# Single loads between GpSimd's copies, earlier weight sums and interleaved exponentials in a fused attention and feed-forward kernel

## The chip, the cores and the metric

The kernel runs on one core of a Trainium2 chip. A core has TensorE (PE, matrix products; PEld is its weight load), VectorE (DVE), ScalarE (ACT), GpSimd (POOL) and SyncE (SP, which here only issues transfers), and 16 DMA engines that all queues share. Time is device time of one execution in microseconds, the median of several runs. A profile is one execution of its own, recorded with every instruction.

## The reference

Attention over 8 batches, 12 heads, 448 tokens and head size 64, then a feed-forward layer over the 3584 tokens. Inputs and output are float32; the kernel works in bfloat16 on the inside.

```python
scores = scale * np.matmul(q, k.transpose(0, 1, 3, 2))
scores = scores - np.max(scores, axis=-1, keepdims=True)
attn = np.exp(scores)
attn = attn / (np.sum(attn, axis=-1, keepdims=True) + 1e-09)
attn_out = np.matmul(attn, v)
x = attn_out.transpose(0, 2, 1, 3).reshape(B * S, H * D)      # 3584 x 768
h = x @ w_in                                                  # 768 x 2048
g = np.maximum(0.01 * h, h)
out = g @ w_out                                               # 2048 x 768
```

## The kernel before

**Units.** Attention is cut into 48 units: two heads of one batch each, six units to a batch. For a unit, q, k and v are loaded as bf16 by GpSimd's queue (`load_soft`, line 137; one load brings two units of one of q, k, v into one of two tiles `fq`, `fk`, `fv`), copied by GpSimd into their places (`cast`, line 162: q and k into a tile `qkb`, v into `v`), and q and k are turned (transposed) into `qkT`: for units below 15 by PE and a copy on DVE (`transposes`, line 250, copy on line 263), later by transposing DMAs in SP's queue (`turn`, line 239). Keys come in four chunks of 112, so a unit has four chunks; chunk 54, say, is unit 13's third. A *burst* (line 788) is the scores of three chunks on PE, one into each of three PSUM slots `sc`, and three exponentials on ACT (`expo`, line 281). `rows` (line 759) multiplies a unit's exponentials with v, and DVE divides (lines 774, 775) into `x`, which is turned into `xT`: by PE and DVE for units 9 to 11 (line 321), by SP's queue for the others.

**Feed-forward.** Tokens go in seven blocks, cut at `cuts` (line 41). The later blocks use a Strassen-like scheme with seven products instead of eight, in `hidden` (x times w_in, line 440) and `block_pair` (h times w_out, line 520). It needs sums and differences of the weights, made once on DVE: `mix_w_in` (line 377; 12 differences, an empty step, 4 additions; called `ins`) and `mix_weights` (line 359; 16 differences and sums; called `outs`). Each is a generator: a `next` puts one more of them into DVE's queue. `mix_h` (line 430) makes two such operations on the hidden values h.

**The stage around the change.** The first block has 640 tokens and is computed in the plain way. `head` (line 591) does 448 of them: 16 groups m of six matmuls into one of two PSUM banks `g`, each followed by a Prelu on ACT (line 600). `neck` (line 611) does the other 192: eight groups of twelve matmuls with a Prelu each (line 651). `second(0)` (line 902) then does the block's products with w_out, with `block_pair`'s steps x counted 0 to 15 in each of two pairs c. After each step `place` (line 846) puts attention work between: by a clock of its own it estimates when a PSUM slot is free (line 877) and then emits a burst, a unit's rows or a turn on PE. A burst in head and neck also calls `feed` (line 826), which emits GpSimd's copies of one unit's q and k, then v's that are owed (`pay`), then the loads that have become allowed (`fetch`), then SP's turn of a unit. In head and neck a burst is `lazy`: its third exponential is kept in `late` and goes out after the next Prelu (`settle`, line 339). All engines run their queues in order. After every copy of units from 12 on, GpSimd writes one element to a tile `gate` (line 174).

Of the kernel before, what the change touches and what calls it, by code (L numbers as in the profile page):

```python
# [16 lines left out]
def kernel(  # L17
# [9 lines left out]
    nc = tc.nc  # L27
# [4 lines left out]
    HP = H // 2  # L32
# [129 lines left out]
    def cast(u, parts=(0, 1, 2), by=nc.gpsimd.tensor_copy):  # L162
        if u >= NU:
            return
        for x in parts:
            f = raw[u].pop(x)
            if x < 2 and u not in qk_sb:
                qk_sb[u] = cast_pool.tile([SC, 2, NSC, 2, D], BF16, name="qkb")
            if x < 2:
                by(qk_sb[u][:, x].rearrange("p so h d -> p h so d"), f)  # L170
            else:
                by(v_sb[u % NV][:, :, :, :D], f)  # L172
            if u >= 2 * HP:
                nc.gpsimd.memset(gate[:, :1], 0.0)

    w_steps = []
    for i in range(4):
        w_steps.append((w_in_sb[:, :, ts(i, DF // 4)], w_in_v[:, :, ts(i, DF // 4)]))
# [157 lines left out]

    late = []

    def settle():
        while late:  # L340
            expo(*late.pop(0))

    open_t = {}
    opened = (0, 1)
# [246 lines left out]
    def head(ins, outs):  # L591

        for m in opened:
            part(0, m, (KD - 1,))
        for m in range(MD):
            if m not in opened:
                part(0, m, range(KH))
                yield KH * HEAD / 2400, False
                part(0, m, range(KH, KD))
            nc.scalar.activation(h[:, m, :HEAD], open_t.pop(m)[:, :HEAD], AX.Prelu, alpha=0.01)  # L600
            settle()
            if m == opened[-1]:
                slots.append(idle)
            if m >= 4:
                next(ins)
            if m >= 14:
                next(outs)
                next(outs)
            yield (KH if m not in opened else 1) * HEAD / 2400, True

    def neck(outs):

        n = cuts[1] - HEAD
        at = place_of(HEAD)
        ms = [x + y for x in range(0, MH, 2) for y in (0, MH)]
        held = {}

        def part2(m, kks):
            fresh = m not in held
            if fresh:  # L620
                held[m] = next_bank()
            for j in range(2):
                for kk in kks:
                    nc.tensor.matmul(  # L624
                        held[m][:, j * n:(j + 1) * n], w_in_sb[:, kk, ts(m + j, P)], xT[:, kk, at:at + n],
                        start=(fresh and j == 0 and kk == 0), stop=(kk == KD - 1), skip_group_check=True,
                    )

        assert all(u == need[1] - 1 for u, _ in owed_x), owed_x
        def after(x):  # L630
            if x % 2:
                mix_h(0, ms[x - 1])
            for _ in range((1, 1, 1, 1, 1, 1, 1, 1)[x]):
                next(outs)

        for m in ms[:2]:
            part2(m, range(KD - 1))
        yield 4 * (KD - 1) * n / 2400, False
        for x, m in enumerate(ms):
            if x < 2:  # L640
                assert rows_done >= need[1], rows_done
                settle_x()
                part2(m, (KD - 1,))
                if x:
                    after(x - 1)
            else:
                part2(m, range(KH))
                after(x - 1)
                yield 2 * KH * n / 2400, False
                part2(m, range(KH, KD))  # L650
            nc.scalar.activation(
                h[:, m:m + 2, HEAD:cuts[1]], held.pop(m)[:, :2 * n].rearrange("p (m t) -> p m t", m=2), AX.Prelu, alpha=0.01
            )
            settle()
            yield 2 * (KH if x > 1 else 1) * n / 2400, True
        model["free"][id(slots[0])] = model["now"] + 1.5
        transposes(NPE - 1, next_slot()[:, 0])
        after(len(ms) - 1)
# [72 lines left out]
    sums, more = mix_w_in(), mix_weights()  # L731
    chunk = 4 * HP + 3
    rows_done = HP
    to = {"pe": HP + 2, "turn": NPE, "cast": HP + 4, "v": HP + 4, "load": [HP + 8] * 3}
    tick = 0

    def advance():
# [47 lines left out]

        return u < to["pe"] or to["pe"] == NPE and u < to["turn"]

    def burst(lazy=False):
        nonlocal chunk
        todo = [divmod(chunk + x, NSC) for x in range(3) if chunk + x < NU * NSC]  # L790
        assert rows_done > todo[-1][0] - NE and turned(todo[-1][0]) and to["v"] > rows_done
        for a, c in todo:
            scores(a, c)
        for a, c in todo[:2] if lazy else todo:
            expo(a, c)
        if lazy:
            late.extend(todo[2:])
        chunk += len(todo)

    X_PE = (HP + 3, HP + 4, HP + 5)  # L800
# [9 lines left out]

    ahead = 0

    def fetch():
        for x, y in enumerate(("cast", "cast", "v")):
            u = to["load"][x]
            if u <= ahead and u - 3 < to[y]:
                load_soft(u, 2, (x,))
                to["load"][x] += 2

    def pay():  # L820
        while owed_v and owed_v[0] < rows_done + NV:
# [4 lines left out]
    def feed(g):  # L826
        nonlocal ahead
        t, r = divmod(g, 4)
        u = 3 * t
        if r < 3:  # L830
            cast(u + 3 + r, (0, 1))
            owed_v.append(u + 3 + r)
            to["cast"] = u + 4 + r
        pay()
        if r < 3:
            ahead = u + 5 + r
            fetch()
            load_w({9: 1, 10: 3}.get(g, 0))
        if r > 0:
            dma_transposes(u + 2 + r)  # L840
            to["turn"] = max(to["turn"], u + 3 + r)
# [1 line left out]
    plan = [9, 8, 8, 8, 8, 5, 0]  # L843
    model = {"now": 0.0, "act": 0.0, "free": {}, "ready": {}}

    def place(i, want, soon=0, full=True, calm=True, first=False, lazy=False, keen=NU, cap=NU):

        free, ready = model["free"], model["ready"]
        done, state = 0, 0
        while True:  # L850
            settle_x(model["now"])
            now = model["now"]
            last = divmod(chunk + 2, NSC)[0]
            blocked = rows_done <= min(last, NU - 1) - NE
            u = rows_done
            whole = u < chunk // NSC
            at = [free.get(id(x), 0.0) for x in slots]
            u = to["pe"]
            if full and max(want, soon) > done and u <= min(last, NPE - 1) and state == 0:
                transposes(u)  # L860
                to["pe"] += 1
                state = 1
                model["now"] += 0.45
                continue
            if want > done and state < 2 and turned(last) and not blocked and len(slots) == 3 and all(
                x <= now + 0.05 + 0.2 * j for j, x in enumerate(at)
            ):
                state = 2
                order = list(slots)
                start = chunk  # L870
                burst(lazy)
                if first:
                    feed(start // 3)
                done += 1
                for x, t in enumerate(order[:chunk - start]):
                    model["act"] = max(model["act"], now + 0.45 + 0.2 * x) + 0.8
                    free[id(t)] = model["act"] + (0.65 if lazy and x == 2 else 0.15)
                    if (start + x) % NSC == NSC - 1:
                        ready[(start + x) // NSC] = model["act"] + 0.1
                model["now"] = now + 0.78  # L880
                continue
            u = to["pe"]
            if first and full and state == 0 and u < min(NPE - 1, to["cast"] - 1) and u - NQ < chunk // NSC and model["act"] <= now + 0.6:
                transposes(u)
                to["pe"] += 1
                state = 1
                model["now"] += 0.45
                continue
            u = rows_done
            if calm and whole and not (lazy and late) and at[0] <= now + 0.05 and ready.get(u, 0) <= now + 0.05 and (  # L890
                u <= (chunk + 5) // NSC - NE or u < keen
            ) and u < cap:
                t = slots[0]
                rows()
                if first:
                    pay()
                model["now"] = now + 1.08
                free[id(t)] = now + 2.33
                continue
            return done  # L900

    def second(i):
# [4 lines left out]
        for c in range(len(spots(i)[1])):  # L907
            for x, _ in enumerate(block_pair(i, c)):
# [3 lines left out]
                    model["now"] += 0.65  # L912
                left -= place(i, left, calm=x not in (1, 3), keen=need[min(i + 2, NR)], cap=NU if all(summed) else need[i + 2])
                if i == 0 and x % 2:
                    next(outs if c == 0 and x < 12 else ins, None)
                for y in range(2):
                    if fresh[y] is None and i + 1 < NR and rows_done >= need[i + 2] - 1 + y:
                        fresh[y] = model["now"] + 7.0
# [15 lines left out]
    for steps, aims, cost in ((head(ins, outs), early, 0.55), (neck(outs), goals, 0.5)):  # L934
        groups = 0
        base = len(early) if aims is goals else 0
        for used, full in steps:
# [2 lines left out]
                groups += 1  # L940
                model["act"] = max(model["act"], model["now"]) + cost
            soon = base + sum(x <= groups + 1 for x in aims) - done if full else 0
            done += place(0, base + sum(x <= groups for x in aims) - done, soon, first=True, lazy=True, full=full, keen=NU if aims is goals or groups > 13 else 0)
    settle()
    assert done == len(early) + len(goals), (done, chunk, rows_done)
    assert to["pe"] == NPE - 1, to
# [44 lines left out]
```

## Time and profile before

| what | value |
| --- | --- |
| runs | 394.15, 394.39, 396.0 us, median 394.39 |
| profiled execution | 392.24 us, of which the span of instructions is 390.4 |
| granted TensorE clock | 1.00 throughout |
| busy | PE 378.1, ACT 265.2, DVE 235.0, POOL 143.4 us |
| head, neck, first output stage | about 31 to 64, 64 to 76, 76 to 110 us |
| GpSimd's copy, its load issue, its memset | 0.62-0.70, 0.70, 0.10 us each |

The span runs from the first to the last instruction; the execution's time is a little longer. A row of a timeline gives start, duration, engine, line, operation, output and inputs, shapes and the number of instructions merged; square brackets show how long the engine had stood idle before it and what ended the wait. A duration on DVE or POOL includes time in which the operation was held up inside the engine.

### The profile page before, as it was taken

The numbers are of one execution on the slowest core, as the hardware profiler recorded it, in microseconds if no ns is written. First come the engines' busy times: TensorE is split into PE (matmuls) and PEld (weight loads), VectorE is DVE, ScalarE is ACT, GpSimd is POOL, SyncE is SP. The second block draws the span as 40 slices with busy tenths as digits, with TensorE's granted clock in tenths as the row PEclk, the third lists the DMA queues.
The fourth block names the chain that finished last, engine by engine and source line by source line (L and its number), as shares of the span: only waits on it lengthen the run. The fifth ranks groups of instructions, "written<-read, shape, count | busy, mean of one in ns | idle before, by whom it ended". The sixth has DMA issues, their size and how long they took to land.

```text
span 390.4 us, 10108 instructions
## 1 busy us (share of the span) xinstructions
PE 378.1 (97%) x4086; PEld 259.3 (66%) x4086; DVE 235.0 (60%) x494; ACT 265.2 (68%) x391; POOL 143.4 (37%) x330
## 2 busy tenths in 40 slices
PE   8899998879999999999999999999999999999996
PEld 3565656755678655886557865579755796568854
DVE  3662636895665745667459574575745666464853
ACT  6998884747678777677765877667867677708700
POOL 8798730976247142460426404354042000000000
PEclk9999999999999999999999999999999999999999
DMA  9999999898999929991399912899228610421023
GB/s 135 199 200 204 170 180 189 100 162 127 181 130 148 128 49 165 184 168 28 71 155 177 165 26 50 174 177 147 35 57 166 138 27 3 106 52 55 3 76 87
DMA packets 93247, 46.75 MB, mean 120 GB/s; under 512 B 51856, under 2 KB 89872, under 8 KB 93200
## 3 DMA queue, kind: packets, MB, share of 16 engines
q0 software_dynamic: 38224, 22.58, 44.5%
q1 hardware_dynamic: 54912, 23.50, 31.8%
q8 instruction: 32, 0.52, 0.6%
q14 instruction: 15, 0.12, 0.1%
q10 hardware_dynamic: 64, 0.02, 0.0%
HBM read 45.61 MB, written 11.01 MB: 145 GB/s over the span
## 4 chain that ended last, share of the span: by engine, by line
PE 87%; DVE 4%; DMA 4%; ACT 2%; issue 1%; POOL 1%; DVEq 0%; POOLq 0%; ACTq 0%
PE g L537 31%; PE g L465 14%; PE sc L465 14%; PE sc L768 11%; PE sc L274 9%; PE g L354 3%; DMA xT<-x 2%; DMA w_in_mix<-in_k_dram 2%; PE g L293 2%; PE g L624 1%; ACT e L283 1%; PE g L257 1%; DVE hmix L437 1%; POOL w_in_mix L141 1%; PE sc L354 1%
## 5 line engine op out<-in xcount | busy, mean ns | idle before, releaser
L283 ACT ACTIVATE e<-sc 112x896 bf16<-112x896 f32 x192 | 162.9, 918 | 51.1 <-PE sc L274 51.0
L537 PEld LDWEIGHTS <-h 128*128 128x128 bf16 x680 | 61.3, 98 | 49.0 <-issue 13.8
L537 PE MATMUL g<-w_out_sb,h 128*128 128x384 bf16 x448 | 84.6, 326 | 0.0
L454 ACT ACTIVATE h<-c 128x512 bf16<-128x512 f32 (+1 forms) x72 | 43.5, 611 | 25.2 <-DVE c L480 16.5
L465 PEld LDWEIGHTS <-w_in_sb 128*128 128x128 bf16 x576 | 54.3, 98 | 6.4 <-issue 0.5
L170 POOL COPY qkb<-fq 112x512 bf16<-112x512 bf16 x38 | 24.2, 637 | 78.5 <-DMA fq<-in_q_dram 40.4
L274 PE MATMUL sc<-qkT 64*128 64x448 bf16 x384 | 49.9, 353 | 2.7 <-DVE qkT L263 2.4
L768 PEld LDWEIGHTS <-e 112*128 112x128 bf16 x1344 | 46.6, 98 | 8.4 <-ACT e L283 6.7
L768 PE MATMUL sc<-v,e 112*128 112x65 bf16 x1344 | 50.1, 194 | 0.3 <-ACT e L283 0.3
L172 POOL COPY v<-fv 112x512 bf16<-112x512 bf16 x38 | 23.6, 624 | 68.4 <-PE sc L768 68.3
L465 PEld LDWEIGHTS <-w_in_mix 128*128 128x128 bf16 x432 | 41.2, 98 | 4.1
L537 PE MATMUL g<-w_mix,h 128*128 128x384 bf16 (+1 forms) x224 | 41.6, 323 | 1.3 <-DVE o L542 1.3
L542 DVE COPY o<-g 128x384 f32<-128x384 f32 x53 | 29.3, 554 | 18.9 <-PE g L537 18.3
L545 DVE TENSOR_TENSOR o<-o,g 128x384 f32<-128x384 f32 x42 | 23.1, 551 | 19.3 <-PE g L537 19.3
L774 DVE RECIPROCAL rec<-sc 112x8 f32<-112x8 f32 x42 | 8.7, 207 | 42.8 <-PE sc L768 41.7
L274 PEld LDWEIGHTS <-qkT 64*128 64x128 bf16 x384 | 15.0, 94 | 28.8 <-issue 18.9
L170 POOL COPY qkb<-fk 112x512 bf16<-112x512 bf16 x38 | 26.5, 697 | 17.4 <-DMA fk<-in_k_dram 17.4
L775 DVE TENSOR_TENSOR x<-sc,rec 112x512 bf16<-112x512 f32 x42 | 29.0, 691 | 1.5
L465 PE MATMUL g<-xT,w_in_sb 128*128 128x256 bf16 (+1 forms) x216 | 28.5, 268 | 0.2 <-DVE o L545 0.2
L465 PE MATMUL sc<-xT,w_in_sb 128*128 128x256 bf16 (+1 forms) x216 | 28.5, 268 | 0.0
L537 PE MATMUL g<-w_mix,hmix 128*128 128x384 bf16 x112 | 21.4, 327 | 0.0
L465 PE MATMUL sc<-x_mix,w_in_mix 128*128 128x256 bf16 (+1 forms) x144 | 19.0, 268 | 0.0
(100 smaller groups left out, 471.2 us busy)
## 6 DMA issues: line engine op xcount, KB each, us to landing
fq<-in_q_dram POOLq DMA_DIRECT2D x19, 224.0 KB, 5.9
fk<-in_k_dram POOLq DMA_DIRECT2D x19, 224.0 KB, 6.3
fv<-in_v_dram POOLq DMA_DIRECT2D x19, 224.0 KB, 5.8
w_in_sb<-in_moe_w_in_dram POOLq DMA_DIRECT2D x4, 768.0 KB, 11.5
w_out_sb<-in_moe_w_out_dram POOLq DMA_DIRECT2D x4, 768.0 KB, 19.3
out_dram<-o SPq DMA_DIRECT2D x7, 336.0 KB, 3.3
out_dram<-o SPq DMA_DIRECT2D x8, 288.0 KB, 3.6
out_dram<-o SPq DMA_DIRECT2D x7, 240.0 KB, 3.2
```

Of the source, the lines that this page charges most:

```text
L170: by(qk_sb[u][:, x].rearrange("p so h d -> p h so d"), f)
L172: by(v_sb[u % NV][:, :, :, :D], f)
L274: nc.tensor.matmul(ps[:, j, :S], t[j * D:(j + 1) * D, S + c * SC:S + c * SC + P], t[j * D:(j + 1) * D, :S], start=True, stop=True,)
L283: nc.scalar.activation(e[:, :, c, :], sc_t.pop((u, c))[:SC, :, :S], AX.Exp, scale=scale)
L354: nc.tensor.matmul(open_t[m][:, :n], w_in_sb[:, kk, ts(m, P)], xT[:, kk, at:at + n], start=(fresh and kk == kks[0]), stop=(kk == KD - 1),)
L454: nc.scalar.activation(hs[:, m:m + 2, cols], x.rearrange("p (m t) -> p m t", m=2), AX.Prelu, alpha=0.01)
L465: nc.tensor.matmul(ps[:, j * nh:(j + 1) * nh], w[:, kk, ts(j, P)], x[:, kk], start=(first and j == 0 and kk == 0), stop=(kk == KH - 1), sk ...
L537: nc.tensor.matmul(ps[:, cols], x[:, m], w[:, m], start=(first and m == 0), stop=(m == MH - 1), skip_group_check=True,)
L542: by(o[:, at], ps[:, :NW])
L545: nc.vector.tensor_add(o[:, at], o[:, at], ps[:, :NW])
L768: nc.tensor.matmul(ps[:, j, qc, :], e[:, at:at + P], vt[:, j, c, :], start=(c == 0), stop=(c == NSC - 1),)
L775: nc.vector.tensor_mul(x_t[u].rearrange("p q j d -> p j q d"), ps[:SC, :, :, :D], rec.to_broadcast([SC, 2, NSC, D]))
```

## The change

1. `cast` loses the write to `gate`.
2. `feed` emits q's copy, then at most one allowed load, then k's copy, then at most one. q's progress has its own counter `to["q"]`, so a load of q needs only q's copies. From burst 16 of the count in `feed` (the neck's two bursts) the loads are allowed one unit sooner (`ahead`). In effect the loads of units 18 and 19 come after the copies of q, k and v of unit 15 instead of three in a row after those of unit 16.
3. The w_in differences go to the middle of groups m = 5 to 10, two each (before: one after each Prelu from m = 4). The w_out sums start in the middle of m = 13 (1, 2, 2) and go on with 2, 2, 1, 1, 2, 1, 1, 1 in the neck (before: 2, 2 after the Prelus of m = 14 and 15, one per step in the neck, four in `second(0)`). Standing in the middle of a group, they come behind the copies of turned q and k that follow the group before. `second(0)` has only the w_in additions left, from its first steps.
4. In the neck a burst emits one exponential and keeps two; each Prelu lets one out. The planner counts the second and third slot as taken longer.

```diff
@@ cast
             else:
                 by(v_sb[u % NV][:, :, :, :D], f)
-            if u >= 2 * HP:
-                nc.gpsimd.memset(gate[:, :1], 0.0)
@@
-    def settle():
-        while late:
+    def settle(n=3):
+        while late and n:
             expo(*late.pop(0))
+            n -= 1
@@ head
                 part(0, m, range(KH))
+                for _ in range(2 if 5 <= m < 11 else 0):
+                    next(ins)
+                for _ in range({13: 1, 14: 2, 15: 2}.get(m, 0)):
+                    next(outs)
                 yield KH * HEAD / 2400, False
...
             settle()
             if m == opened[-1]:
                 slots.append(idle)
-            if m >= 4:
-                next(ins)
-            if m >= 14:
-                next(outs)
-                next(outs)
@@ neck
-            for _ in range((1, 1, 1, 1, 1, 1, 1, 1)[x]):
+            for _ in range((2, 2, 1, 1, 2, 1, 1, 1)[x]):
                 next(outs)
...
-            settle()
+            settle(1)
@@
-    to = {"pe": HP + 2, "turn": NPE, "cast": HP + 4, "v": HP + 4, "load": [HP + 8] * 3}
+    to = {"pe": HP + 2, "turn": NPE, "q": HP + 4, "cast": HP + 4, "v": HP + 4, "load": [HP + 8] * 3}
@@ burst
-        for a, c in todo[:2] if lazy else todo:
+        assert not late
+        for a, c in todo[:3 - lazy]:
             expo(a, c)
-        if lazy:
-            late.extend(todo[2:])
+        late.extend(todo[3 - lazy:])
@@ fetch
-    def fetch():
-        for x, y in enumerate(("cast", "cast", "v")):
+    def fetch(n=3):
+        for x, y in enumerate(("q", "cast", "v")):
             u = to["load"][x]
-            if u <= ahead and u - 3 < to[y]:
+            if n and u <= ahead and u - 3 < to[y]:
                 load_soft(u, 2, (x,))
                 to["load"][x] += 2
+                n -= 1
@@ feed
         if r < 3:
-            cast(u + 3 + r, (0, 1))
+            if g >= 16:
+                ahead = u + 6 + r
+            for x, y in enumerate(("q", "cast")):
+                cast(u + 3 + r, (x,))
+                to[y] = u + 4 + r
+                fetch(1)
             owed_v.append(u + 3 + r)
-            to["cast"] = u + 4 + r
         pay()
         if r < 3:
-            ahead = u + 5 + r
+            ahead = max(ahead, u + 5 + r)
             fetch()
@@ place
-                    free[id(t)] = model["act"] + (0.65 if lazy and x == 2 else 0.15)
+                    free[id(t)] = model["act"] + (0.15, 0.15 + 0.5 * (lazy > 1), 0.15 + 0.5 * lazy)[x]
@@ second
-                    next(outs if c == 0 and x < 12 else ins, None)
+                    next(ins, None)
@@ around head and neck
-            done += place(..., lazy=True, ...)
+            done += place(..., lazy=2 if aims is goals else 1, ...)
```

More of the change, by code (lines that the diff above doesn't have):

```diff
@@ L786, in turned, with burst @@
         return u < to["pe"] or to["pe"] == NPE and u < to["turn"]
-    def burst(lazy=False):
+    def burst(lazy=0):
         nonlocal chunk
@@ L844, with place @@
     model = {"now": 0.0, "act": 0.0, "free": {}, "ready": {}}
-    def place(i, want, soon=0, full=True, calm=True, first=False, lazy=False, keen=NU, cap=NU):
+    def place(i, want, soon=0, full=True, calm=True, first=False, lazy=0, keen=NU, cap=NU):
         free, ready = model["free"], model["ready"]
@@ L942 @@
             soon = base + sum(x <= groups + 1 for x in aims) - done if full else 0
-            done += place(0, base + sum(x <= groups for x in aims) - done, soon, first=True, lazy=True, full=full, keen=NU if aims is goals or groups > 13 else 0)
+            done += place(0, base + sum(x <= groups for x in aims) - done, soon, first=True, lazy=2 if aims is goals else 1, full=full, keen=NU if aims is goals or groups > 13 else 0)
     settle()
```

## The prediction

> **What bounds the kernel now.** The page comes first. TensorE (PE) is busy 97% of a span of 390.4 us, no other engine over 68%, so only PE's idle time, 390.4 - 378.1 = 12.3 us, can be won.
>
> ```profile
> PE 378.1 (97%) x4086; PEld 259.3 (66%) x4086; DVE 235.0 (60%) x494; ACT 265.2 (68%) x391; POOL 143.4 (37%) x330
> ```
>
> The table by stretches then says where it lies. Its columns are the stretch, its length, busy time (and instructions) of each engine, granted clock, DMA share and GB/s.
>
> ```profile
> 55.00:60.00 5.00, 4.57 (x71) 3.02 (x72) 2.64 (x7) 3.11 (x5) 0.00 (x0) 1.00 1.19 176
> 60.00:65.00 5.00, 4.25 (x56) 3.12 (x53) 4.33 (x11) 1.09 (x2) 0.00 (x0) 1.00 1.20 207
> 65.00:70.00 5.00, 4.32 (x48) 3.41 (x47) 3.10 (x7) 3.94 (x7) 1.75 (x5) 1.00 0.81 110
> 75.00:80.00 5.00, 3.26 (x32) 1.91 (x30) 4.79 (x7) 3.03 (x5) 5.00 (x12) 1.00 0.99 106
> 80.00:85.00 5.00, 3.71 (x52) 2.31 (x50) 4.83 (x8) 2.84 (x4) 3.09 (x9) 1.00 1.39 199
> 160.00:200.00 40.00, 40.00 (x437) 28.94 (x434) 24.44 (x48) 28.81 (x44) 13.64 (x35) 1.00 0.75 123
> ```
>
> From 55 to 85 us PE idles 0.43 + 0.75 + 0.68 + 1.74 + 1.29 = 4.9 us; from 160 on it idles almost nowhere. The rest is at both ends. PE's timeline of that stretch names the waits, in square brackets:
>
> ```profile
> 59.45 1.10 PE L768 MATMUL sc<-v,e 112*128 112x65 bf16 x29 [0.34 <-ACT e L283]
> 64.00 1.98 PE L624 MATMUL g<-xT,w_in_sb 128*128 128x192 bf16 x22 [0.76 <-DVE qkT L263]
> 68.55 1.84 PE L624 MATMUL g<-xT,w_in_sb 128*128 128x192 bf16 x18 [0.64 <-ACT h L651]
> 78.94 0.36 PE L274 MATMUL sc<-qkT 64*128 64x448 bf16 x2 [1.74 <-DVE qkT L263]
> 83.32 0.81 PE L537 MATMUL g<-w_mix,h 128*128 128x384 bf16 x4 [1.28 <-DVE o L542]
> ```
>
> The last four, 0.76 + 0.64 + 1.74 + 1.28 = 4.42 us, are what the change touches. VectorE's (DVE's) timeline shows what its copies queued behind:
>
> ```profile
> 61.80 0.55 DVE L388 TENSOR_TENSOR w_in_mix<-w_in_sb,w_in_mix 128x768 bf16<-128x768 bf16 x1
> 62.27 0.55 DVE L366 TENSOR_TENSOR w_mix<-w_out_sb 128x768 bf16<-128x768 bf16 x1
> 62.85 0.56 DVE L368 TENSOR_TENSOR w_mix<-w_mix,w_out_sb 128x768 bf16<-128x768 bf16 x1
> 63.33 0.62 DVE L263 COPY qkT<-g 128x896 bf16<-128x896 bf16 x1
> ...
> 74.64 2.23 DVE L437 TENSOR_TENSOR hmix<-h 128x512 bf16<-128x512 bf16 x1
> ...
> 78.26 0.62 DVE L263 COPY qkT<-sc 128x896 bf16<-128x896 bf16 x1
> ...
> 81.24 0.54 DVE L371 TENSOR_TENSOR w_out_sb<-w_out_sb 128x768 bf16<-128x768 bf16 x1
> 81.70 1.09 DVE L549 TENSOR_TENSOR h<-h 128x1024 bf16<-128x1024 bf16 x1
> 82.72 0.54 DVE L542 COPY o<-g 128x384 f32<-128x384 f32 x1
> ```
>
> Two things: sums of 0.47 us net stand ahead of copies that PE waits for, and the L437 at 74.64, which takes 0.42 us elsewhere, took 2.23 because GpSimd (POOL) copied without a break from 73.05 to 76.60.
>
> **Sums of weights (lines 591-634, 914).** The 12 w_in sums go two at a time to m = 5..10, and end near 50 us instead of 64.6. They need the third and fourth quarter of w_in; the fourth was issued at 30.11 and took 12.2 us, so it is there at 42.3, before the seventh sum (about 45). DVE has 4.06 us idle before 54.10: cost nothing; without that idle time it is 0.47 each.
>
> The w_out sums start at m = 13 instead of 14: one, two, two, then 2, 2, 1, 1, 2, 1, 1, 1 in the neck. At 61.8 no sum is left ahead of the copy: it would run there instead of at 63.33, and the 0.76 would go. But the first sum now reaches DVE's head near 55.9 and needs the second quarter of w_out, which was issued at 40.59:
>
> ```profile
> w_out_sb<-in_moe_w_out_dram POOLq DMA_DIRECT2D x1, 768.0 KB, 17.9
> ```
>
> It lands at 40.59 + 17.9 = 58.5. Three sums then run to about 60.1, and behind them wait the reciprocal (59.12 before) and product for unit 10, whose x PE transposes at 60.39. That product ends near 61.0 instead of 60.0, PE's transposes slip 0.6, unit 11's and m = 15 follow. So of the 0.76 I take 0.1, with 0 and 0.76 as ends (an arrival 1 us later would cost 1 more).
>
> In the first output stage the four sums at 81.24, 83.19, 86.11, 87.88 are gone and the w_in additions come at steps 3, 5, 7, 9; the sum before L549 (0.46 us) has no successor.
>
> **Exponentials (lines 339, 654, 788-798, 877).** ACT ran two exponentials (66.40, 1.72 us) before the second Prelu (68.00), which frees the bank for the 68.55 matmuls. One now runs before it: Prelu near 67.2, PE ready at 67.8. From then Prelu 0.40 + exponential 0.82 alternate against PE groups of 1.03 us; following both leaves one wait of 0.08 for the fifth group. I take 0.56 of the 0.64 (0 to 0.64). The planner moves two things as its slots stay taken 0.5 and 1.0 us longer: after the first half of the fifth group the third slot is 0.71 ahead of its clock where 0.45 is let through (before 0.21), so the burst 51-53 goes half a group later, and unit 12's rows one group later (one exponential still owed). PE has other work in both places: nothing on PE. Unit 12's x now stands between the two mix_h and two sums on DVE, about 1.5 us before the copy of unit 14.
>
> **Loads, copies, memset (lines 173, 813-842).** Each of 108 memsets goes; copies 0.59 apart become 0.55 apart: 0.035 x 108 = 3.8 us of POOL, which is 37% busy and waits 68.3 us for PE and 95 us for DMAs. Cost and gain nothing beside PE; it is on the path only from 67.8 to 81. There the order was q14 k14, loads, v13, load, v14, q15 k15 v15 q16 k16, three loads, v16. Now unit 18's loads come after q15, k15 and v15, each 0.70 plus a wait for the copy just ahead, whose tile it overwrites (the row of such a load: 0.26, at 72.35). So k15 ends near 75.8 (was 74.84), k16 near 79.6 (76.60), k17 near 81.3 (80.9): the turns of 15 and 16, in SP's queue in the order 15, x of 12, 16, 17, go out at 75.8 and 79.6 (74.86 and 78.15). Unit 18's q comes sooner, which ends POOL's wait at 81.43. In exchange DVE finds 0.96 us without a copy three times between 74 and 78.4. L437 for the fifth pair starts near 71.6-72.2, against one copy instead of three; the copy of unit 14 then runs near 75.1-75.7, as PE reaches its third scores near 76.1. Wait of 1.74: gone, 1.7; if POOL still holds L437 up for two copies it is 0.55-1.1 less, so 0.6 to 1.74. At L549/L542, PE would ask near 79.1; DVE's chain mix_h, one sum, L549, L542 from 75.7 with one blocked copy ends near 78.7. Take 1.2 of 1.28 (0.4 to 1.28).
>
> [...]
>
> **Sum.** 0.1 + 0.56 + 1.7 + 1.2 = 3.56 us by 83 us. Later places may take some back. Unit 16's turn is needed near 87.5 (second chunk of the burst at 90.86, so 91.1, less 3.6); sent at 79.6 with the 7.0 us it took before it lands at 86.6, 0.9 early. Turns took between 3.8 us (that of 15) and 9.0 (after 97): 0 to 1.1 lost. At the start of the second block DVE waits until 108.96 for a turned x sent at 101.09 (7.9 us), then joins, then PE starts at 110.12. It will be sent near 97.4, behind the turn of 21; with 7.9 us PE starts near 106.4, 3.7 sooner; with 9.6 us (the longest turn between 70 and 130) 2.0 sooner. I take 0.36 off: net 3.2. Profiled: span 387.2, time 392.24 - 3.2 = 389.0. That execution was 2.15 below the median 394.39; on the median's scale 391.2.
>
> **The rivals.** *The second block holds the gain back.* The turned x lands where it did, since the loads of 22 (95.59 and 96.29, landing after 8.0 and 10.0 us) fill the DMA engines. For: DMA share 1.15 there; against: 0.71 and 0.88 in 85-95, room to move up. Gain 0 to 2.0: 393.4. *The w_out arrival or POOL's copies eat it*: w_out 1 us later (-1), L437 and L549 still blocked (-0.8): gain 1.4, 393.0. For: 2.23 in the row; against: loads now break POOL's run. *Slower*: the turn of 16, behind POOL's three loads and waits, comes so late that PE stands at burst 63-65. It costs one for one from 87.5, wipes out the gain if it lands at 91.1, and is 0.5% slower from 93.1, 13.5 us after being sent. For: loads of 14 took 19.2-20.2 us behind w_out; against: no turn in 70-130 took over 9.6. If it lands at 95: 394.4 + 3.9 = 398.3. *No effect*, gain 0: needs all four waits to be replaced; nothing speaks for it.
>
> **How the numbers follow.** The forecast 0.60 (its own range 390.0 to 392.2); second block 0.18; w_out or copies 0.12; slower 0.07; no effect 0.03. A measurement of this kernel tells about 0.5%, 2.0 us. Faster takes the forecast, a third of w_out or copies, a quarter of second block: 0.69; slower 0.08; same 0.23. Low: all 4.42 us and 0.4 for the runs' own spread (394.15 to 396.0), 389.6; high: the second block's 0 with nothing won, 394.3.
>
> **What would show it.** DVE with a wait for w_out near 56-58.5 and L624 starting near 63.9; the neck's ACT row alternating L651 and L283; L263 for unit 14 before 76 and no wait over 0.3 at its scores; L542 before 79.2; PE's first L465 near 106.4. Wrong if L437 is again over 1.5 us, if PE waits for a turn (qkT) near 87, or if L465 starts at 110.

## The result, and the profile after

The changed kernel takes 392.23 us, the kernel before 394.35 (medians of 22 executions each, taken in turn): ratio 0.9952, 95% interval 0.9933 to 0.9972. (The ratio is made of fast executions alone, without one of the changed kernel at 395.96 us, and is not the quotient of the medians.) That is 2.1 us by the medians; the forecast was 3.2, and 391.2 on a scale where the kernel before had 394.39.

The two profiled executions hardly differ: 392.14 us against 392.24, spans 390.2 and 390.4. So the profile has to be read for two things: where the 3.56 us expected by the third product went, and why the medians moved when the profiles did not.

From the table by stretches of the changed kernel (stretch, length, busy time and instructions of PE, PEld, DVE, ACT, POOL, then granted clock, DMA share, GB/s):

```profile
60.00:65.00 5.00, 4.40 (x54) 3.33 (x51) 4.64 (x12) 1.09 (x2) 0.00 (x0) 1.00 1.23 206
65.00:70.00 5.00, 4.97 (x56) 3.90 (x55) 3.13 (x7) 4.30 (x8) 2.64 (x4) 1.00 0.64 85
75.00:80.00 5.00, 2.44 (x13) 0.81 (x11) 4.76 (x10) 2.50 (x4) 4.68 (x6) 0.84 1.38 128
80.00:85.00 5.00, 5.00 (x52) 2.62 (x51) 3.47 (x6) 2.25 (x4) 4.11 (x6) 0.81 0.94 161
```

The neck (65 to 70) has become full. But 75 to 80 holds less PE work than before (2.44 against 3.26 us), and the granted clock, 1.00 everywhere in the profile before, is 0.84 and 0.81. PE's timeline of the changed kernel, with the waits in brackets:

```profile
63.64 1.98 PE L621 MATMUL g<-xT,w_in_sb 128*128 128x192 bf16 x22
66.22 3.50 PE L621 MATMUL g<-xT,w_in_sb 128*128 128x192 bf16 x38
...
75.48 0.36 PE L271 MATMUL sc<-qkT 64*128 64x448 bf16 x2
77.76 0.36 PE L271 MATMUL sc<-qkT 64*128 64x448 bf16 x2 [1.92 <-DVE x L772]
78.77 0.56 PE L271 MATMUL sc<-qkT 64*128 64x448 bf16 x2 [0.64 <-DVE qkT L260]
79.25 3.38 PE L535 MATMUL g<-w_out_sb,h 128*128 128x384 bf16 x12
82.57 0.74 PE L271 MATMUL sc<-qkT 64*128 64x448 bf16 x6
83.24 0.82 PE L535 MATMUL g<-w_mix,h 128*128 128x384 bf16 x4
```

PE starts the neck at 63.64 (64.00 before), runs through it without the 0.64, and is at the scores of the burst 54-56 at 75.48 instead of 76.65: 1.17 us won. There it waits 1.92 us for unit 12's x, whose slot chunk 55 needs, and 0.64 for the copy of unit 14: 2.56 in place of 1.74. Then twelve matmuls that took 2.12 us before take 3.38; before, their row was

```profile
79.23 2.12 PE L537 MATMUL g<-w_out_sb,h 128*128 128x384 bf16 x12
```

The wait of 1.28 before the third product is gone, and the product starts at 83.24 instead of 83.32. Microsecond by microsecond the clock shows why the twelve took longer:

```profile
77.00:78.00 1.00, 0.24 (x2) 0.09 (x1) 0.98 (x2) 0.00 (x0) 1.00 (x2) 1.00 1.35 117
78.00:79.00 1.00, 0.36 (x4) 0.10 (x2) 1.00 (x3) 0.79 (x1) 1.00 (x2) 0.72 1.78 94
79.00:80.00 1.00, 1.00 (x5) 0.41 (x4) 0.90 (x3) 0.77 (x2) 1.00 (x2) 0.50 1.55 126
80.00:81.00 1.00, 1.00 (x5) 0.47 (x4) 0.92 (x2) 0.28 (x1) 0.26 (x1) 0.50 1.43 191
81.00:82.00 1.00, 1.00 (x6) 0.45 (x4) 1.00 (x3) 0.00 (x0) 0.85 (x2) 0.57 1.36 226
82.00:83.00 1.00, 1.00 (x10) 0.40 (x8) 0.70 (x2) 0.00 (x0) 1.00 (x2) 1.00 0.92 199
```

PE's pause begins at 75.84; the clock falls near 78.4, with two matmuls in between, and is back near 81.9: 3.4 us at 0.50. VectorE's timeline shows why unit 12's x was late; its reciprocal could have started when PE's rows ended near 73.5, and started at 76.79:

```profile
58.41 0.56 DVE L364 TENSOR_TENSOR w_mix<-w_out_sb 128x768 bf16<-128x768 bf16 x1 [2.61 <-DMA w_out_sb<-in_moe_w_out_dram]
...
71.73 1.80 DVE L366 TENSOR_TENSOR w_mix<-w_mix,w_out_sb 128x768 bf16<-128x768 bf16 x1
73.45 0.55 DVE L369 TENSOR_TENSOR w_out_sb<-w_out_sb 128x768 bf16<-128x768 bf16 x1
73.92 1.09 DVE L435 TENSOR_TENSOR hmix<-h 128x512 bf16<-128x512 bf16 x1
75.11 0.87 DVE L436 TENSOR_TENSOR h<-h 128x512 bf16<-128x512 bf16 x1
75.91 0.95 DVE L369 TENSOR_TENSOR w_out_sb<-w_out_sb 128x768 bf16<-128x768 bf16 x1
76.79 0.19 DVE L771 RECIPROCAL rec<-sc 112x8 f32<-112x8 f32 x1
```

and GpSimd's timeline beside it what held the sums up:

```profile
71.94 0.62 POOL L172 COPY v<-fv 112x512 bf16<-112x512 bf16 x1
72.48 0.62 POOL L170 COPY qkb<-fq 112x512 bf16<-112x512 bf16 x1
73.40 0.70 POOL L141 DMA_DIRECT2D fq<-in_q_dram  x1 [0.30 <-POOL qkb L170]
74.10 0.62 POOL L170 COPY qkb<-fk 112x512 bf16<-112x512 bf16 x1
```

The sum at 71.73 lasts until 73.53, 0.43 after the second of two copies; the L435 at 73.92 until 75.01, 0.3 after the next one. Elsewhere they take 0.55 and 0.42. It isn't always VectorE that stands: a later copy of GpSimd's is stretched from 0.62 to 1.19 us while VectorE's product and sum at 77.02 and 77.63 run at their usual 0.69 and 0.55.

```profile
77.45 1.19 POOL L170 COPY qkb<-fq 112x512 bf16<-112x512 bf16 x1
```

### The profile page after: what moved, and what is told of

It reads as the page before. It is cut to its first block, busy times and chain, and to the rows that moved or that the text cites. A ratio compares the mean times of both kernels' runs of the same rounds, so it can differ in the third digit from the quotient of the medians.

```text
span 390.2 us, 10005 instructions
## 1 busy us (share of the span) xinstructions
PE 379.7 (97%) x4086; PEld 259.9 (67%) x4086; DVE 234.7 (60%) x494; ACT 265.2 (68%) x391; POOL 139.0 (36%) x222
## 4 chain that ended last, share of the span: by engine, by line
PE 81%; DMA 9%; DVE 4%; POOL 2%; issue 1%; ACT 1%; DVEq 0%; POOLq 0%; ACTq 0%
PE g L535 34%; PE g L463 13%; PE sc L463 13%; PE sc L765 10%; PE sc L271 8%; DMA w_out_sb<-in_moe_w_out_dram 5%; DMA fk<-in_k_dram 3%; DMA w_in_mix<-in_k_dram 2%; POOL qkb L170 1%; PE g L290 1%; POOL w_in_mix L141 1%; ACT e L280 1%; DVE w_mix L364 1%; DVE w_mix L366 1%; PE g L254 0%
## 5 line engine op out<-in xcount | busy, mean ns | idle before, releaser
L535 PE MATMUL g<-w_out_sb,h 128*128 128x384 bf16 x448 | 85.8, 330 | 0.0
L172 POOL COPY v<-fv 112x512 bf16<-112x512 bf16 x38 | 24.6, 651 | 68.7 <-PE sc L765 68.5
L540 DVE COPY o<-g 128x384 f32<-128x384 f32 x53 | 29.3, 554 | 20.5 <-PE g L535 19.9
L170 POOL COPY qkb<-fk 112x512 bf16<-112x512 bf16 x38 | 24.6, 648 | 21.6 <-DMA fk<-in_k_dram 21.6
L463 PE MATMUL g<-x_mix,w_in_mix 128*128 128x256 bf16 (+1 forms) x144 | 19.0, 268 | 0.0
```

What stands on the lines that cost most here:

```text
L463: nc.tensor.matmul(ps[:, j * nh:(j + 1) * nh], w[:, kk, ts(j, P)], x[:, kk], start=(first and j == 0 and kk == 0), stop=(kk == KH - 1), sk ...
L535: nc.tensor.matmul(ps[:, cols], x[:, m], w[:, m], start=(first and m == 0), stop=(m == MH - 1), skip_group_check=True,)
L540: by(o[:, at], ps[:, :NW])
```

## The experiments

After the result: theory A says that the sums and mix_h queued ahead of unit 12's reciprocal and unit 14's copy, held up by GpSimd's copies, made PE wait, and that the pause lowered the clock. Rival B says that unit 12's rows come too late because the planner moved them a group back. Ratios below are to the kernel before, run in turn with each.

**The sums put back** (label u_sums).

```diff
-                for _ in range(2 if 5 <= m < 11 else 0):
-                    next(ins)
-                for _ in range({13: 1, 14: 2, 15: 2}.get(m, 0)):
-                    next(outs)
...
+            if m >= 4:
+                next(ins)
+            if m >= 14:
+                next(outs)
+                next(outs)
...
-            for _ in range((2, 2, 1, 1, 2, 1, 1, 1)[x]):
+            for _ in range((1, 1, 1, 1, 1, 1, 1, 1)[x]):
...
-                    next(ins, None)
+                    next(outs if c == 0 and x < 12 else ins, None)
```

> The changed kernel with the weight sums back in their old places (one w_in difference after each Prelu from m = 4, w_out sums from m = 14, four of them in the first output stage); loads, copies and exponentials as changed. Theory A (in the changed kernel VectorE is late at the end of the neck because sums and mix_h stand ahead of unit 12's reciprocal while GpSimd copies): the wait of 1.92 us on x of unit 12 shrinks to under 1.0, and the waits at the first L621 (0.76) and at the third product (up to 1.3) return; time 392.0 to 393.2. Rival B (unit 12's rows come one group too late through the kept exponentials): the wait of 1.9 stays, the others come on top; 393.3 to 394.4.

392.68 us (12 executions), 0.9952 (0.9921 to 0.9982): within A's span, and not to be told from the changed kernel. There was no wait on unit 12's x, 0.64 for unit 14's copy, and 0.8 each at the neck's first matmuls and at the third product, which started at 81.84. From the neck's first matmul to the third product this run takes 17.10 us, the changed kernel 19.60, of which 1.3 are the lower clock. So the new order of the sums won 0.8 us at the neck and lost more than that behind it. PE's timeline also shows the first rival of the prediction, the second block:

```profile
110.66 1.42 PE L463 MATMUL g<-xT,w_in_sb 128*128 128x256 bf16 x6 [2.24 <-DVE o L543]
```

Behind this wait the clock is at 0.50 again, from 110.7 to 114.1 (0.83 in the mean of 110 to 120).

**The exponentials put back** (u_lazy).

```diff
-            settle(1)
+            settle()
...
-            done += place(..., lazy=2 if aims is goals else 1, ...)
+            done += place(..., lazy=1, ...)
```

> The changed kernel with the neck's exponentials as before (two at once, one kept, all let out at the next Prelu); everything else as changed. A: unit 12's rows stand a group earlier, its x is ready in time, but the copy of unit 14 is still behind mix_h and sums, so PE waits 1 to 2 us there in place of the 1.92 + 0.64, and 0.64 at the Prelu returns: 392.0 to 392.9. B: the wait at the scores after 75 us is under 0.5 us and the kernel gains 1.5: 390.4 to 391.2.

394.24 us (12), 1.0018 (0.9990 to 1.0046): 2.0 us more than the changed kernel by the medians, 2.6 by the ratios, above both expectations. B falls: with the rows a group earlier PE waits longer. VectorE's timeline of this run, then PE's:

```profile
77.38 2.46 DVE L372 TENSOR_TENSOR w_mix<-w_out_sb,w_mix 128x768 bf16<-128x768 bf16 x1
79.77 0.61 DVE L260 COPY qkT<-sc 128x896 bf16<-128x896 bf16 x1
```

```profile
80.43 0.36 PE L271 MATMUL sc<-qkT 64*128 64x448 bf16 x2 [4.04 <-DVE qkT L260]
```

The last sum ahead of unit 14's copy met a run of three copies (77.70 to 79.43) and took 2.46 us; at 77.63 in the changed kernel it took 0.55. With the exponentials as changed the reciprocal and product of unit 12, which PSUM feeds (0.19 and 0.69 us in both runs), stand between the sums, and the run of copies begins at 77.45, beside the product, with the stretched copy of 1.19. So what the exponentials are worth hangs on where VectorE's queue meets GpSimd's; the 0.64 at the Prelu is the smaller part.

**The loads put back, three in a row** (u_loads).

```diff
-            if g >= 16:
-                ahead = u + 6 + r
-            for x, y in enumerate(("q", "cast")):
-                cast(u + 3 + r, (x,))
-                to[y] = u + 4 + r
-                fetch(1)
+            cast(u + 3 + r, (0, 1))
             owed_v.append(u + 3 + r)
+            to["cast"] = u + 4 + r
```

with `fetch` as before.

> The changed kernel with the loads three in a row after the copies of unit 16, as before; no memset. A: GpSimd copies without a break again, VectorE is held up longer between 72 and 76, PE waits 2.5 to 4 us in all at the scores of the burst 54-56: 392.8 to 394.0. B: no difference to the changed kernel within 0.5: 391.8 to 392.7.

393.91 us (12), 0.9979 (0.9944 to 1.0013). The median is in A's span, but the interval overlaps that of the changed kernel, so the time alone does not decide; the trace does. One VectorE operation of 0.55 us stood for 4.00, over six copies that followed each other without a load, and ended at 76.24, 0.46 after the first load's issue began. VectorE's timeline of this run, and then GpSimd's:

```profile
72.24 4.00 DVE L366 TENSOR_TENSOR w_mix<-w_mix,w_out_sb 128x768 bf16<-128x768 bf16 x1
```

```profile
72.45 0.62 POOL L172 COPY v<-fv 112x512 bf16<-112x512 bf16 x1
73.00 0.62 POOL L170 COPY qkb<-fq 112x512 bf16<-112x512 bf16 x1
...
75.22 0.60 POOL L170 COPY qkb<-fk 112x512 bf16<-112x512 bf16 x1
75.78 0.70 POOL L141 DMA_DIRECT2D fq<-in_q_dram  x1
```

PE waited 4.00 and 0.45 us at the scores, against 1.92 and 0.64 in the changed kernel.

**Openings without the earlier loads** (gap). To u_loads, three tiny transfers are added:

```diff
+    def gap(g, y):
+        if g == 16:
+            nc.gpsimd.dma_start(out=gate[32 * y:32 * y + 16, :], in_=q[0, 0, :16, :2])
...
+            for y in range(2):
+                cast(u + 3 + r, (y,))
+                gap(g, y)
...
         pay()
+        gap(g, 2)
```

> The kernel of u_loads (the changed kernel with the loads three in a row after unit 16's copies) with three tiny transfers of 16 x 2 elements, issued by GpSimd after the copies of unit 15's q, k and v into a tile that nobody reads: the openings between the copies without the earlier loads. A (what counts is that a transfer's issue stands between two copies and lets VectorE in): the w_out sum that took 4.00 us in u_loads takes under 2.0, PE's waits at the scores of 54-56 fall from 4.45 to under 3.0, 391.8 to 393.0. Rival (what counts is that the loads of unit 18 come sooner): 393.4 to 394.4, the waits near 4.

The sum that took 4.00 takes 2.05, and PE waits 2.65 + 0.54, both a little over A's bounds of 2.0 and 3.0 and far from the rival's 4. The openings do what A says of the mechanism. The time, 393.41 (12), 0.9975 (0.9954 to 0.9995), lies on the rival's side of the line and cannot be told from u_loads: the twelve executions of u_loads reach from 390.2 to 396.6. How much of the loads' 1.7 us is the opening is thus shown for the hold in the trace, not for the time.

**The memset put back** (u_gate: the two lines in `cast`).

> The changed kernel with the one-element memset after each of GpSimd's copies from unit 12 on, as before. A: a memset of 0.1 us between two copies lets VectorE in no more than none does, GpSimd is up to 0.5 us later at 79: 391.8 to 392.8. Rival (the memset is an opening for VectorE, and taking it out cost time): VectorE's longest w_out sum near 72 us falls from 1.80 to under 1.0, and 391.0 to 391.7.

392.10 us (10), 0.9948 (0.9922 to 0.9975): no difference. The sum near 72 us stood for 1.84, and PE's waits at the scores were 2.19 and 0.45. The memset is no opening here (1.84 us with it, 1.80 without), and costs nothing that these times show.

**PE kept busy in its pause** (warm).

```diff
         for x, (a, c) in enumerate(todo):
             scores(a, c)
+            if chunk == 54 and x < 2:
+                for _ in range((8, 3)[x]):
+                    nc.tensor.matmul(banks[1], w_in_sb[:, 0, :P], w_in_sb[:, 0, :512], start=True, stop=True)
```

> The changed kernel with eleven extra 128x512 matmuls (8 behind the scores of chunk 54, 3 behind those of chunk 55) into the bank that is not in use; their products are thrown away. A with the clock as its second half (PE's pause near 76 to 78.8 makes the chip grant half the clock for some 3 us, which costs 1.3): granted clock 1.00 in the record, 390.6 to 391.4. Rival (the lower clock is not caused by the pause, or costs nothing): clock as low as in the changed kernel, time 392.2, or up to 1.7 more where the pause is shorter than the extra matmuls.

390.85 us (12), 0.9932 (0.9903 to 0.9960). The trace is that of the changed kernel up to 75.5; then (L794 are the extra matmuls):

```profile
75.54 0.36 PE L271 MATMUL sc<-qkT 64*128 64x448 bf16 x2
75.83 1.90 PE L794 MATMUL g<-w_in_sb 128*128 128x512 bf16 x8
77.83 0.37 PE L271 MATMUL sc<-qkT 64*128 64x448 bf16 x2
78.12 0.82 PE L794 MATMUL g<-w_in_sb 128*128 128x512 bf16 x3
78.88 0.36 PE L271 MATMUL sc<-qkT 64*128 64x448 bf16 x2
79.17 2.12 PE L536 MATMUL g<-w_out_sb,h 128*128 128x384 bf16 x12
81.23 0.74 PE L271 MATMUL sc<-qkT 64*128 64x448 bf16 x6
81.90 0.82 PE L536 MATMUL g<-w_mix,h 128*128 128x384 bf16 x4
```

VectorE is as late as ever, but the clock stays at 1.00, the twelve matmuls take 2.12 again, and the third product starts at 81.90: 1.34 us sooner than in the changed kernel. That is the price of the lower clock in this trace; the medians differ by 1.38.

**The same in the kernel before** (b_warm: eight such matmuls behind the scores of chunk 55, in the unchanged kernel).

> The kernel before with eleven of the extra matmuls cut to eight, all behind the scores of chunk 55, where PE waits 1.74 us for the copy of unit 14; products thrown away. A with the clock: in most executions of the kernel before PE's pause there lowers the clock as well (its records show 0.994 on average), so the clock rises to 0.998 or more and the median falls 0.6 to 1.5 us. Rival: the kernel before loses its clock elsewhere, clock near 0.994, time same or up to 0.3 longer.

392.84 us (12) against 394.67, 0.9967 (0.9947 to 0.9986); the mean granted clock of its executions is 0.998, that of 84 executions of the kernel before 0.994. Below 0.998 are 3 of these 12 executions, and 66 of those 84. So the kernel before loses its clock in that pause too, in most executions, but not in the one that was profiled. The profile of this run also shows that the pause itself varies. VectorE's and PE's timelines:

```profile
71.37 3.97 DVE L438 TENSOR_TENSOR h<-h 128x512 bf16<-128x512 bf16 x1
```

```profile
80.55 0.36 PE L274 MATMUL sc<-qkT 64*128 64x448 bf16 x2 [1.18 <-DVE qkT L263]
```

Here it was an L438 that stood, across six copies with a memset behind each, and the third scores began 3.0 us after the end of the second, against 1.74 in the profile before; the wait at the third product was 0.20 in place of 1.28.

**Sums taken out of the neck** (defer).

```diff
-            for _ in range((2, 2, 1, 1, 2, 1, 1, 1)[x]):
+            for _ in range((2, 2, 1, 1, 1, 0, 0, 0)[x]):
...
-                    next(ins, None)
+                    if c or x > 1:
+                        next(outs if c == 0 and x < 10 else ins, None)
```

> The changed kernel with four w_out sums taken out of the neck: 2, 2, 1, 1, 1, 0, 0, 0 there, the last four in the first output stage at steps 3, 5, 7, 9 of the first pair, and the w_in additions after them. A (sums queued ahead of unit 12's reciprocal and unit 14's copy, held up by GpSimd's copies, make PE wait): the waits at the scores of 54-56 fall from 2.56 to under 1.0 us, granted clock 1.00 in the profile, 390.2 to 391.4. Rival (GpSimd's copies hold up whatever stands at VectorE's head, so that fewer sums do not help): waits still 2 or more, 392.0 to 392.6.

388.51 us (6), 0.9870 (0.9835 to 0.9905), better than expected and better than both kernels. PE's timeline from 70 to 112 us shows two waits over 0.1 us in all:

```profile
76.38 0.36 PE L271 MATMUL sc<-qkT 64*128 64x448 bf16 x2 [0.17 <-DVE qkT L260]
...
108.65 0.81 PE L463 MATMUL g<-xT,w_in_sb 128*128 128x256 bf16 x6 [2.54 <-DVE o L543]
```

A is shown: three sums fewer ahead of unit 14's copy take the waits from 2.56 to 0.17. The gain is then so large that the second block's turned x becomes the bound, and 2.54 us are given back there: VectorE stood for that x with the join behind it that frees PE's bank.

```profile
107.71 0.43 DVE L415 TENSOR_TENSOR x_mix<-xT 128x512 bf16<-128x512 bf16 x1 [5.17 <-DMA xT<-x]
```

**Two sums earlier instead** (early: `(4, 2, 1, 1, 1, 1, 0, 1)` in the neck).

> The changed kernel with the neck's w_out sums as 4, 2, 1, 1, 1, 1, 0, 1: two more in VectorE's pause near 65 to 67 us, fewer behind 71. A: the waits at the scores of 54-56 fall by about 1 us, 390.9 to 391.9. Rival: unchanged, 392.0 to 392.6, or the four sums delay mix_h and the neck, 392.6 to 393.4.

389.92 us (6), 0.9904 (0.9867 to 0.9940), better than expected. The waits at the scores fall to 0.57 + 0.17; 0.92 stays at the third product, since a mix_h took 2.05 us across three copies.

**The second block.** In defer_x the sums over turned x go behind the last joins; in defer_x_early the neck's sums are `(4, 2, 1, 0, 0, 0, 0, 0)` as well.

```diff
-                        fresh[y] = model["now"] + 7.0
+                        fresh[y] = model["now"] + (12.0 if i == 0 else 7.0)
```

> The kernel of defer with the sums over turned x for the second block (L415) put after the last joins of the first output stage instead of among them. C (the wait of 2.54 us at the second block's first product is VectorE standing at L415 for the turned x while the join that frees the bank is queued behind it): that wait falls under 0.6 us, part of it returns at the third product of the block, which needs the sums: 386.6 to 388.0. Rival (the turned x is needed at once anyway, since a product waits for it a moment later): 388.2 to 388.9.

> As defer_x with the neck's w_out sums as 4, 2, 1, 0 and none after, so that VectorE has one sum less behind 71 us. A: the copy of unit 14 is up to 0.5 us sooner and the remaining wait at the scores is gone, 386.4 to 387.8; Rival (VectorE is no longer late there): the same as defer_x within 0.4.

389.47 (6), 0.9874 (0.9842 to 0.9906), and 389.16 (6), 0.9859 (0.9820 to 0.9898). The wait for the bank was gone, but the products with the sums then waited 1.5 and 1.9 us for them: the rival was right, the turned x is needed at once, though both medians lie above the spans expected for defer_x. In defer_x_early the waits at the scores are gone altogether (0.35 in defer_x). Neither time differs from defer.

**Why that x is late** (defer_gap: defer with the loads and openings of gap). In every profile with single loads the turn of unit 15 landed late. The rows of its transfer, in the kernels before, after, gap and defer in this order (microseconds from issue to landing at the end):

```profile
qkT<-qkb SPq DMA_TRANSPOSE x1, 3.8
```

```profile
qkT<-qkb SPq DMA_TRANSPOSE x1, 6.3
```

```profile
qkT<-qkb SPq DMA_TRANSPOSE x1, 3.6
```

```profile
qkT<-qkb SPq DMA_TRANSPOSE x1, 7.4
```

It is 3.2 to 3.8 in the five kernels with three loads in a row and 6.3 to 7.6 in the nine others, where unit 18's loads are under way with it. GpSimd's copy of unit 17's q waits for it (in defer 2.19 us, until 82.16), and the loads behind slip.

> The kernel of defer with the loads and openings of gap: unit 18's loads three in a row after unit 16's copies, and three tiny transfers between unit 15's copies. D (in the kernels with single loads unit 15's turn shares the DMA engines with unit 18's loads and lands 6 to 7.5 us after it is sent instead of 3.8; GpSimd's copy of unit 17's q waits for it, all later loads and turns slip, and the second block's first product waits): the copy of unit 17's q does not wait, the wait at the second block's first product falls from 2.54 to under 1.3 us, while the waits at the scores of 54-56 grow to 0.5 to 1.5; 387.4 to 389.0. Rival (the second block's turn is late for the DMA engines' load there alone): that wait stays at 2 or more, 388.6 to 390.

390.28 us (6), 0.9898 (0.9862 to 0.9935). The copy of unit 17's q did not wait, the wait of 2.54 at the second block was gone, and 0.89 + 0.17 came at the scores, as D has it; the rival falls in the trace. The time is above both spans, and its median is not below that of defer. What the single loads give VectorE they seem to take from the turns, with the opposite balance in the other order; the times cannot weigh the two.

## Why the prediction was right or wrong, point by point

**Right.** The direction and the range of 389.6 to 394.3 held; the forecast's own range, 390.0 to 392.2, was just missed. Of the four waits, *0.76*: the first w_out sum waited on VectorE until 58.4 for the transfer (58.5 was worked out), PE's turn of unit 10 waited 0.56 (0.6), and the neck began 0.36 sooner (0.1 was taken). *0.64*: gone, with ACT alternating Prelu and exponential. *1.28*: gone as a wait. The memset was worth nothing.

**The step that failed** is the 1.7 us for the scores, "L437 ... against one copy instead of three; the copy of unit 14 then runs near 75.1-75.7". It costed the hold for one operation. Of the five operations in that queue from 71.73 on, four were held: two sums (1.80 and 0.95 for 0.55) and both parts of mix_h (1.09 and 0.87 for 0.42); the fifth, the sum at 73.45, took its 0.55. And unit 12's x, put some 1.5 us before a copy at 75.1 to 75.7, came with a reciprocal at 76.79, the copy of unit 14 at 78.09. The waits grew by 0.82 instead of shrinking by 1.7, outside the bounds of 0.6 to 1.74. It had no row for chunk 55 waiting on x at all. This is the rival "POOL's copies eat it", to which 0.12 was given and 0.8 us as its price for L437 and L549; at the scores alone it was 2.5. The row of 2.23 us before speaks for more as well: from 74.64 to 76.87 it spanned the rest of one copy and three more (from 74.82, 75.41 and 76.00), where the lower bound of 0.6 allows for two.

Of the signs that were named, the wait for w_out and the alternating ACT row came. The copy of unit 14 before 76, L542 before 79.2 and the second block's first product near 106.4 did not: 78.09, 81.36 (there L540) and 109.78.

**A term was missing:** the clock. The pause lowered it, and 1.34 us were lost (warm), about as much as the fourth wait had given. That is why the profiles are alike.

**Why the medians still moved by 2.1** was not in the prediction either. It took the profile before as typical but for an offset of 2.15. Of 84 executions of the kernel before, the 18 with a mean clock of 0.998 or more have a median of 392.3, the others 394.7. The profiled execution, with 392.24 us and a clock of 1.00, was like the 18. b_warm shows that keeping PE busy in that one pause brings the median down 1.8 us (0.33% by the ratio). The forecast of 3.2 was therefore near 2.1 partly by luck: between the two profiles nothing was won, and the profile before was some 2 us better than a usual execution. No trace shows an execution of the kernel before at the lower clock, so how the 2.1 divides among the waits stays open. In the parts, by the medians (by the ratios): undoing the loads cost 1.7 us (1.1), the exponentials 2.0 (2.6), the sums 0.4 (0.0), the memset none; only the exponentials can be told from none by their times.

Not every loss of clock belongs to this stage. The profiles of u_sums, defer, defer_x_early and defer_gap also show 0.50 for 3.4 us between 11 and 16 us, long before anything that was changed (mean clock of these executions 0.991, 0.996, 0.991 and 0.994; in defer every stretch from 55 to 120 us is at 1.00). One profile against another can therefore differ for a reason that has nothing to do with the edit; waits within a stage can be compared, ends of the span less so.

**Second block.** It held gains back where PE came sooner: 2.24 in u_sums, 2.54 in defer, 1.04 in early; u_loads, which was late, waited 1.15 too. In the changed kernel PE was no sooner there, the x landed in time, and it cost nothing. The turn of 16 made PE wait in none of the profiles.

## What to carry to other kernels

Where two engines hold each other up, cost the whole queue that stands ahead of the operation that PE needs, not the one long row; and shorten that queue before anything else: moving four sums out of the neck (defer) was worth more than the four edits of the change together, 3.7 us against 2.1 by the medians. Look at the granted clock of more than one execution before taking a profile as the base of a sum: here a pause of 2.24 us on PE was followed by a clock of 0.50 (u_sums) and one of 2.54 was not (defer), and filling the pause at the scores was worth some 1.3 to 1.8 us (warm, b_warm).

## What the runs showed of the hardware

- A VectorE sum that takes 0.55 us elsewhere took 4.00 over a run of six GpSimd copies (u_loads), and ended 0.46 us after GpSimd began to issue a transfer (0.70 us); with three issues of 0.48 to 0.51 us between the copies it took 2.05 (gap). A memset between the copies did not do that: an operation of 0.43 us took 3.97 across six copies (b_warm). In the profile after, the w_out sums took 0.55 to 1.80 us and mix_h 0.42 to 1.10, while the operations that PSUM feeds kept their lengths (reciprocal 0.19 to 0.21, product 0.69, the output's copy and join 0.54 to 0.56). Other copies were the ones to stand, 1.19 us for 0.62 (changed kernel, 77.45); no run shows what decides it.
- PE's clock fell to 0.50 for 3.4 us in a pause of 2.56 us with two matmuls in it (changed kernel) and at the end of one of 2.24 wholly idle (u_sums, second block); from the pause of 2.19 us in u_gate on it stayed low for 6.8 (0.75 and 0.56 in the means of 75 to 80 and 80 to 85). It did not fall at a pause of 2.54 us in defer (1.00 in the means of 100 to 110 and 110 to 120). No run shows why one pause lowers the clock and a longer one does not.
- The transposing transfer of unit 15 took 3.2 to 3.8 us where the three loads of 224 KB came behind it in a row, and 6.3 to 7.6 where they were issued one by one within about 4 us around it.
